# An attention and mixture-of-experts kernel on one core: expert weights halved in pieces of 512 columns, and the tables of the left rows begun after two batches

## The chip, the cores and the metric

One Trainium2 chip, one of its cores. The metric is the device time of one execution in microseconds. The kernel before was timed three times: 989.87, 989.98 and 990.37 us, median 989.98 us. A traced execution of it took 992.81 us, of which 991.0 us lie between its first and its last instruction (its span).

## What is computed

The reference has two stages. The first is attention through 49 agents, the second a mixture of eight experts of which each row uses one:

```python
a2k = sm(agents, k); agent_v = a2k @ v          # per batch: 49 x 128
x = sm(q, agents) @ agent_v                     # 4 batches x 11456 rows x 128
logits = x @ w_gate; e_idx = argmax(logits)     # 8 experts
gate_w = softmax(logits)[e_idx]
eom = sigmoid(x @ w_output_gate)[e_idx]
for e in range(8):                              # rows with e_idx == e
    out[rows] = gate_w * eom * (relu(x[rows] @ w1[e]) @ w2[e])
```

`w1` is 128 x 1024 and `w2` 1024 x 128 for each expert. Matmuls that must be exact beyond fp16 are made as a sum of fp16 products: a value is split in a high half (rounded to fp16) and a low half (the rest), and the product of the two low halves is dropped.

## The kernel before, in words

**Two ways to a result.** In each batch one expert is chosen by far the most often (`choose`, L886). All rows of the batch go through that expert in the main stream: 92 tiles of up to 512 rows (23 a batch), each with 16 `h` products of 512 columns (`mm1`, L1283), eight relu steps that split `h` in halves `hh` (ScalarE) and `hl` (VectorE) (`relu`, L1307), and `y` products (`mm2`, L1317), which ScalarE and VectorE add up, GpSimd scales by a factor for each row and SyncE stores (`finish`, `store`). The rows that chose another expert, the left rows, are gathered afterwards, computed in tiles of 128 with their own expert's weights, and scattered over the output. They come in two phases (`PHASES`, L30): phase 0 is batches 0 and 1, with 12 tiles, phase 1 is batches 2 and 3, with one.

**The left rows, step by step.** `q_rest` and `q_tail` (L1110, L1217) leave for each batch the running counts of rows for each expert (`cumd`, `tot`) and set `counted` to the number of batches done. `left_prepare(ph)` (L1731) then makes, in this order, the table of the phase (`left_table`, L1436: which tile has which expert, some 23 short VectorE instructions, three small matmuls, three stores), loads the averages of the agents (`left_averages`, L1653) and runs the index work for groups of four tiles (`left_index`, L1505: which rows, by two rounds of indirect DMAs on GpSimd's queue, first of `cumd` and then of the saved exponentials `efd`). Phase 0 begins when three batches are counted, phase 1 when all four are and phase 0's index work is over (`prepared`). `left_static` (L1763) is two streams ("ways"), each of which takes every second tile; in a way a tile's front (`left_load`, L1636, and `left_front`, L1665: double the exponentials on VectorE, transpose `let` and product `lx` on TensorE, halves `lxs`) begins once the tile before it in this way is finished, and its back (`left_back`, L1687: 24 `lh` matmuls, relu, 16 `ly` matmuls, two scalings) follows. The back of phase 1's tile also waits for the end of the main stream (`ended`, L1788). `left_scatter` (L1797) writes a tile's rows out by an indirect DMA.

**Halves.** The left rows need all eight experts' weights in halves. `halves` (L966) makes them, one expert after another, beside the main stream: load `w1` and `w2` of the expert (`hw`), squares with an accumulated sum on ScalarE (`hd`, `hsq`), a sum over partitions by a matmul with ones (`hr`), a power of two as scale (`hb`, `hs`), then for each of the two weights: multiply by the scale in place (ScalarE, fp32, 1024 columns), copy to fp16 (ScalarE, 1024), subtract (GpSimd, 1024, fp32 minus fp16 to fp16), store. Experts 0 to 2 may begin once the first batch's weights are ready, 3 to 5 with the second's, 6 and 7 with the third's; `choose` waits while an expert is in the making, and left rows begin only when all eight are made.

**What sets the order.** No engine's order is found by hand. The program is written as generators ("streams", `spawn`) that ask for one instruction at a time; a planner with a model of costs (`Clock`, L56) walks through time and grants a request when its operands are ready by the model. Streams with a smaller priority number are asked first: -1 for what opens the next batch, 0 for relu and finish, 1 for the phase 0 preparation, 2 by default, 3 for the halves and the scatters, 4 for fronts and scores, 5 for the ways. The order on each engine is fixed when the program is built; on the chip each engine goes through its own list and waits on semaphores.

Of the kernel before, what the change touches and what calls it, by code (L numbers as in the profile page):

```python
# [7 lines left out]
F32 = mybir.dt.float32  # L8
F16 = mybir.dt.float16
# [8 lines left out]
P = 128  # L18
# [250 lines left out]
def agent_attention_top1_moe(ctx, tc, qT, kT, v, aT, wg, wo, w1, w2, cst, sides, out):  # L269
# [696 lines left out]
    def halves():  # L966

        for e in range(E):
            while not (clk.started and len(state) > e // 3 and "i12" in state[len(state) - 1]
                       and (len(state) < B and K.get(len(state), {"v": 0})["v"] < 8) and not urgent[0]):  # L970
                yield None
            halving[0] = True
            src, dst = [], []
            for x in (w1, w2):
                s = wk.tile([P, F], F32, name=f"hw{len(src)}_{e}", tag="w1t", bufs=2)
                yield from SY.q.dma_start(s, x[e])
                src.append(s)
            sq = wk.tile([P, 2], F32, name=f"hsq{e}", tag="hsq")
            for k in range(2):
                d = wk.tile([P, 2 * F], F16, name=f"hd{k}_{e}", tag="w2t", bufs=2)  # L980
                yield from ACT.q.activation(d[:, 0:F], src[k], AF.Square, accum_out=sq[:, k:k + 1])
                dst.append(d)
            yield from wait_free()
            r = bank(f"hr{e}")
            mark = hold()
            yield from PE.q.matmul(r[:, 0:2], ones, sq, start=True, stop=True)
            sb, s, si = (wk.tile([P, 2], I32, name=f"h{n}{e}", tag=f"h{n}") for n in ("b", "s", "si"))
            for k, x in enumerate((9, 15)):
                yield from DVE.q.tensor_scalar(sb[:, k:k + 1], r[:, k:k + 1].bitcast(I32), -0.5,
                                               float((190 + x << 23) - (1 << 23)), op0=ALU.mult, op1=ALU.add)  # L990
            release(mark)
            yield from DVE.q.tensor_scalar(s, sb, 0x7F000000 + 0x800000, None, op0=ALU.bitwise_and)
            yield from POOL.q.tensor_scalar(si, s, -1.0, float(254 << 23), op0=ALU.mult, op1=ALU.add)
            s, si = s.bitcast(F32), si.bitcast(F32)
            yield from POOL.q.tensor_tensor(wsi[:, e:e + 1], si[:, 0:1], si[:, 1:2], op=ALU.mult)
            for k, x in enumerate((w1p, w2p)):
                if k == 0:
                    hi, lo, full = dst[k][:, 0:F], dst[k][:, F:2 * F], src[k]
                else:
                    v4 = dst[k].rearrange("p (f h c) -> p f h c", h=2, c=C)  # L1000
                    hi, lo, full = v4[:, :, 0, :], v4[:, :, 1, :], src[k].rearrange("p (f c) -> p f c", c=C)
                yield from ACT.q.activation(full, full, AF.Copy, scale=s[:, k:k + 1])
                yield from ACT.q.copy(hi, full)
                yield from POOL.q.tensor_tensor(lo, full, hi, op=ALU.subtract)
                yield from SY.q.dma_start(x[e], dst[k])
            halved[0] = e + 1
            halving[0] = False
# [654 lines left out]
        while clk.now() < t:  # L1662
            yield None

    def left_front(nm, ef, xt, two, ie, av):  # L1665
        yield from DVE.q.tensor_tensor(xt, ef[:, 0:A].unsqueeze(1).broadcast_to([P, 2, A]),
                                       two.unsqueeze(2).broadcast_to([P, 2, A]), op=ALU.mult)
        yield from wait_free()
        t = bank(f"let{nm}")
        mark = hold()  # L1670
        yield from PE.q.transpose(t[0:2 * A, 0:P], xt.rearrange("p b k -> p (b k)"), idf)
        et = wk.tile([P, P], F32, name=f"let_sb{nm}", tag="l_et")
        yield from ACT.q.copy(et[0:2 * A], t[0:2 * A, 0:P])
        release(mark)
        yield from wait_free()
        x = bank(f"lx{nm}")
        mark = hold()
        yield from PE.q.matmul(x[:, 0:P], av[0:2 * A], et[0:2 * A], start=True, stop=True)
        xs = wk.tile([P, 2, P], F16, name=f"lxs{nm}", tag="l_xs")
        yield from ACT.q.copy(xs[:, 0, :], x[:, 0:P])  # L1680
        yield from DVE.q.scalar_tensor_tensor(xs[:, 1, :], x[:, 0:P], 1.0, xs[:, 0, :], op0=ALU.mult, op1=ALU.subtract)
        release(mark)
        g = wk.tile([P, 1], F32, name=f"lg_{nm}", tag="l_g", bufs=3)
        yield from DVE.q.tensor_tensor(g, ef[:, A:A + 1], ie, op=ALU.mult)
        return xs, g
# [45 lines left out]
    def left_prepare(ph):  # L1731

        b0, nb, nst, _ = PHASES[ph]
        while counted[0] < (3 if ph == 0 else B) or ph and not prepared[0]:
            yield None
        if ph == 0:
            yield from SY.q.dma_start(ls, sides)
        yield from left_table(ph)
        averaged[ph] = yield from left_averages(ph, f"{ph}")
        i = 0  # L1740
        for j, n in enumerate((4, 4, 4) if nst > 2 else (nst,)):
            big = None
            if nst > 2:
                while B - 1 not in K or K[B - 1]["s"] < min(3 * j + 3, NU):
                    yield None
                big = wk.tile([P, min(24, NCOL - 24 * j), A2], F32, name=f"big{ph}_{i}", tag=f"S{j}", bufs=1)
                big = big.rearrange("p t a -> p (t a)")

            def got(k, t, ti, tu, ef, oa, xt, two, ie, i=i):
                ready[ph, i + k] = t, ti, k, tu[:, k:k + 1], ef[:, k, :], oa[:, k, :], xt[:, k], two[:, k, :], ie[:, k:k + 1]  # L1750
            yield from left_index(ph, i, n, f"s{ph}_{i}", got, big)
            i += n
        prepared[0] = True
# [9 lines left out]
    def left_static(way):  # L1763


        while way and (B - 1 not in K or K[B - 1]["v"] < NU):
            yield None
        todo = [(ph, k) for ph, x in enumerate(PHASES) for k in range(x[2])][way::WAYS]
        ops = {}
        finished = [0]  # L1770

        def fronts():
            for i, (ph, k) in enumerate(todo):
                while (ph, k) not in ready or i > finished[0] or halved[0] < E:
                    yield None
                t, ti, kk, _, ef, _, xt, two, ie = ready[ph, k]
                yield from pause(t - clk.now())
                w1t, w2t = yield from left_load(ph, ti, kk, f"{ph}_{k}", left_place)
                yield from pause(max(clk.ready[x.name] for x in (w1t, w2t)) - clk.now())
                xs = yield from left_front(f"{ph}_{k}", ef, xt, two, ie, averaged[ph])  # L1780
                ops[ph, k] = xs, w1t, w2t

        spawn(fronts(), LEFT - 1)
        for ph, k in todo:
            while (ph, k) not in ops:
                yield None
            xs = ops.pop((ph, k))
            while ph == len(PHASES) - 1 and not ended[0]:  # L1788
                yield None
            tu, _, oa = ready[ph, k][3:6]  # L1790
            yield from left_back(f"{ph}_{k}", *xs, oa, ("lh", "ev")[way])
            for x in (f"lw1{ph}_{k}", f"lw2{ph}_{k}"):
                scored((x, 0, 0))
            left.append((ph, oa, tu))
            finished[0] += 1
# [21 lines left out]
                return stop.value  # L1817

    AHEAD = 5
    LASTQ = 0  # L1820
    WARM = 6000
    WARM0 = 36
# [6 lines left out]
    spawn(clear(), 5)  # L1829
    spawn(small_products(), 4)  # L1830
    for ph in range(len(PHASES)):
        spawn(left_prepare(ph), 1 - ph)
    for way in range(WAYS):
        spawn(left_static(way), LEFT)
    spawn(left_scatter(), 3)
    spawn(halves(), 3)
    main_stream()

    DVE.tensor_tensor(more, over[:, 0:1], over[:, 1:2], op=ALU.max)
# [1 line left out]
    with tc.For_i(0, some, 1):  # L1841
        for ph, (b0, nb, nst, rows) in enumerate(PHASES):
            nr = nc.values_load(nti[ph][0:1, 0:1], min_val=0, max_val=rows,
                                skip_runtime_bounds_check_because="at most one tile per 128 tokens and one per group")
            with tc.For_i(nst, nr, 1) as i:
                ti, tu, ef, oa, xt, two, ie = drain(left_index(ph, i, 1, f"d{ph}"))
                w1t, w2t = drain(left_load(ph, ti, 0, f"d{ph}"))
                av = drain(left_averages(ph, f"d{ph}"))
                xs = drain(left_front(f"d{ph}", ef[:, 0, :], xt[:, 0], two[:, 0, :], ie, av))
                drain(left_back(f"d{ph}", xs, w1t, w2t, oa[:, 0, :]))  # L1850
                drain(left_store(ph, oa[:, 0, :], tu[:, 0:1]))

# [62 lines left out]
```

## Time and profile before

| what | value |
|---|---|
| median of three runs | 989.98 us |
| the profiled execution, and its span | 992.81 us, 991.0 us |
| TensorE (PE) busy | 949.1 us, 96% of the span |
| VectorE (DVE) busy | 828.3 us, 84% |
| ScalarE (ACT) busy | 632.2 us, 64% |
| GpSimd (POOL) busy | 394.9 us, 40% |
| mean granted TensorE clock | 0.991 |
| the 16 DMA queues, mean rate | 166 GB/s |

A row of a group gives line, engine, operation, output and inputs, shape and count, then the time in which any instruction of the group ran, the mean of one in ns, and the idle time in front of it with what ended it. Nearly every row says L219, since one helper issues all queued instructions; the names of the tiles tell them apart. TensorE's matmuls are pipelined, so rows of single matmuls are longer than the distance from one to the next.

### The profile page before, as it was taken

To read this page: it belongs to the slowest core of one execution; us is meant where nothing else is said; L and a number is where in the kernel's file an instruction comes from. 1 tells how busy PE (TensorE), PEld (TensorE's weight loads), DVE (VectorE), ACT (ScalarE), POOL (GpSimd) and SP (SyncE) were. 2 spreads that over 40 slices of the span, in tenths; PEclk is the share of its full clock that TensorE was granted. 3 is DMA by queue.
4 is the path that set the end of the run, shared out by engine and by line. 5 is a ranking of instruction groups with operands and counts; after the bars stand their busy time and mean duration, and the time that the engine had idled before them with its cause. 6 is when DMAs were issued, how large, how long until landed. Compare 5 with 4: busy or idle time off the path is not lost.

```text
span 991.0 us, 37853 instructions
## 1 busy us (share of the span) xinstructions
PE 949.1 (96%) x15819; PEld 716.8 (72%) x15819; DVE 828.3 (84%) x2245; ACT 632.2 (64%) x1459; POOL 394.9 (40%) x661
## 2 busy tenths in 40 slices
PE   9999999999999999999989999999999999999994
PEld 7867777777777777777767777777777666767783
DVE  2878888989878988989878889889889898898872
ACT  2378677766767886657767666666556565655542
POOL 1124366652243666432335454432226334533321
PEclk9999999999999999999999999999999999999997
DMA  9996958647469865444676554444332525524341
GB/s 324 302 322 181 249 157 219 183 136 167 152 183 267 245 180 166 129 146 142 179 245 208 161 153 144 145 125 148 84 101 77 134 73 151 133 86 133 94 138 62
DMA packets 112609, 164.10 MB, mean 166 GB/s; under 512 B 62961, under 2 KB 71110, under 8 KB 112432
## 3 DMA queue, kind: packets, MB, share of 16 engines
q1 hardware_dynamic: 111184, 160.18, 54.6%
q8 instruction: 125, 2.05, 0.9%
q0 software_dynamic: 1248, 1.44, 0.8%
q14 instruction: 52, 0.43, 0.2%
HBM read 97.91 MB, written 43.49 MB: 143 GB/s over the span
## 4 chain that ended last, share of the span: by engine, by line
PE 70%; DVE 18%; ACT 7%; DMA 2%; issue 2%; POOL 0%; POOLq 0%; SPq 0%; ACTq 0%; DVEq 0%
PE y L219 36%; PE h L219 17%; DVE hl L219 10%; ACT hh L219 4%; PE ks L219 3%; PE qs L219 3%; PE av L219 2%; PE warm L219 2%; PE ly L219 1%; DVE os L219 1%; ACT hd L219 1%; PE avT L219 1%; PE lh L219 1%; DVE a L219 1%; PE lg L219 1%
## 5 line engine op out<-in xcount | busy, mean ns | idle before, releaser
L219 PE MATMUL y<-vv,hh 128*128 128x256 f16 (+1 forms) x2880 | 526.1, 274 | 12.0 <-DVE lL L219 3.9
L219 DVE SCALAR_TENSOR_TENSOR hl<-h,hh 128x512 f16<-128x512 f32 (+1 forms) x736 | 450.5, 667 | 75.6 <-ACT hh L219 74.0
L219 PE MATMUL y<-vv,hl 128*128 128x128 f16 (+1 forms) x2880 | 500.9, 220 | 3.0 <-DVE hl L219 2.0
L219 ACT ACTIVATE hh<-h 128x512 f16<-128x512 f32 (+1 forms) x736 | 372.6, 593 | 177.9 <-PE h L219 177.9
L219 PEld LDWEIGHTS <-hh 128*128 128x128 f16 (+1 forms) x2880 | 283.6, 98 | 54.8 <-issue 13.7
L219 PEld LDWEIGHTS <-hl 128*128 128x128 f16 (+1 forms) x2880 | 284.8, 99 | 16.7 <-issue 8.2
L219 PE MATMUL h<-x_ld,w 128*128 128x512 f16 (+1 forms) x1472 | 254.5, 376 | 3.2 <-DVE hl L219 2.7
L219 PEld LDWEIGHTS <-w 128*128 128x128 f16 x1472 | 83.5, 95 | 116.6 <-issue 79.3
L219 POOL TENSOR_TENSOR os<-os,smt 128x512 f32<-128x512 f32 (+1 forms) x91 | 94.4, 1038 | 95.4 <-DVE os L219 65.4
L219 ACT COPY ys<-y 128x256 f32<-128x256 f32 x179 | 68.2, 381 | 73.8 <-PE y L219 72.4
L219 DVE TENSOR_TENSOR os<-y,ys 128x256 f32<-128x256 f32 x179 | 74.1, 414 | 17.9 <-ACT ys L219 17.3
L219 POOL TENSOR_TENSOR e<-ef,e 128x392 f16<-128x392 f32 (+1 forms) x48 | 44.3, 923 | 64.1 <-ACT e L219 63.8
L219 POOL TENSOR_TENSOR ev<-S,km_o 128x400 f32<-128x400 f32 (+1 forms) x36 | 32.9, 914 | 54.5 <-PE av L219 52.3
L219 PE MATMUL ks<-at,k_ld 128*32 128x50 f32 (+1 forms) x2252 | 47.2, 213 | 0.9 <-DMA k_ld<-kT 0.7
L219 PEld LDWEIGHTS ks<-at,k_ld 128*32 128x32 f32 (+1 forms) x2252 | 40.6, 117 | 10.3 <-issue 7.0
L219 PE MATMUL qs<-at,q_ld 128*32 128x50 f32 (+1 forms) x2736 | 43.5, 210 | 2.0 <-issue 2.0
L219 PEld LDWEIGHTS qs<-at,q_ld 128*32 128x32 f32 (+1 forms) x2736 | 36.5, 111 | 12.0 <-issue 10.8
L219 POOL TENSOR_SCALAR smt<-lT,i 128x8 f32<-128x8 f32 (+1 forms) x48 | 15.6, 326 | 64.7 <-DVE lT L219 27.5
L219 POOL TENSOR_TENSOR hd<-hw,hd 128x1024 f16<-128x1024 f32 x16 | 34.2, 2137 | 14.0 <-ACT hd L219 14.0
L219 ACT COPY S<-ks 128x400 f32<-128x400 f32 (+1 forms) x48 | 23.7, 498 | 22.5 <-PE ks L219 22.5
L219 POOL TENSOR_TENSOR sm<-sm,ev 128x400 f32<-128x400 f32 (+1 forms) x33 | 32.2, 977 | 11.2 <-ACT ev L219 11.2
L219 PE MATMUL lh<-lxs,lw_ld 128*128 128x128 f16 x312 | 33.7, 225 | 1.8 <-ACT lxs L219 0.7
(294 smaller groups left out, 1127.3 us busy)
## 6 DMA issues: line engine op xcount, KB each, us to landing
v_ld<-v SPq DMA_DIRECT2D x44, 512.0 KB, 4.9
q_ld<-qT SPq DMA_DIRECT2D x44, 512.0 KB, 4.1
out<-os SPq DMA_DIRECT2D x88, 256.0 KB, 3.1
k_ld<-kT SPq DMA_DIRECT2D x43, 512.0 KB, 5.3
efd<-ef SPq DMA_DIRECT2D x44, 200.0 KB, 3.6
x_ld<-x_ld SPq DMA_DIRECT2D x132, 64.0 KB, 3.9
hw<-w SPq DMA_DIRECT2D x16, 512.0 KB, 7.1
lw_ld<-w1p SPq DMA_DIRECT2D x13, 512.0 KB, 4.5
```

The costliest lines, as they stand in the source:

```text
L219: return getattr(self.eng, op)(*a, **k)
```

## The change

Four edits.

1. `halves` works on pieces of 512 columns. A piece gets its own square (ScalarE) and its own column of a sum tile with four columns, which two matmuls add up in place of one. The scaling in place on ScalarE and the copy to fp16 become one ScalarE instruction, which reads the fp32 weights, multiplies by the scale and writes the high half; the fp32 product for the subtraction is made by GpSimd (`tensor_scalar`, in place) ahead of its subtraction. The stream's priority goes from 3 to 6.
2. `left_prepare` of phase 0 begins when two batches are counted, with priority 3 in place of 1. After the table it waits until the weights of the last batch are made (`i12` of batch 3), then loads the averages, and spawns the index work as a stream of its own with priority 1. Phase 1's order stays as it was.
3. The doubling of the exponentials leaves `left_front` for a step of its own, `left_double`, ahead of the load of the tile's weights; a pause of 1 us by the model's clock stands after it.
4. The tiles `let_sb` and `lxs` take buffers of the rings `w1t` and `w2t` in place of rings of their own.

```diff
-            sq = wk.tile([P, 2], F32, name=f"hsq{e}", tag="hsq")
+            sq = wk.tile([P, 4], F32, name=f"hsq{e}", tag="hsq")
             for k in range(2):
-                yield from ACT.q.activation(d[:, 0:F], src[k], AF.Square, accum_out=sq[:, k:k + 1])
+                for hf in range(2):
+                    cs = slice(hf * 512, (hf + 1) * 512)
+                    yield from ACT.q.activation(d[:, cs], src[k][:, cs], AF.Square, accum_out=sq[:, 2 * hf + k:2 * hf + k + 1])
...
-            yield from PE.q.matmul(r[:, 0:2], ones, sq, start=True, stop=True)
+            yield from PE.q.matmul(r[:, 0:2], ones, sq[:, 0:2], start=True, stop=False)
+            yield from PE.q.matmul(r[:, 0:2], ones, sq[:, 2:4], start=False, stop=True)
...
-                yield from ACT.q.activation(full, full, AF.Copy, scale=s[:, k:k + 1])
-                yield from ACT.q.copy(hi, full)
-                yield from POOL.q.tensor_tensor(lo, full, hi, op=ALU.subtract)
+                for hf in range(2):
...
+                    yield from ACT.q.activation(hi, full, AF.Copy, scale=s[:, k:k + 1])
+                    yield from POOL.q.tensor_scalar(full, full, s[:, k:k + 1], None, op0=ALU.mult)
+                    yield from POOL.q.tensor_tensor(lo, full, hi, op=ALU.subtract)
...
-    def left_front(nm, ef, xt, two, ie, av):
+    def left_double(ef, xt, two):
         yield from DVE.q.tensor_tensor(xt, ef[:, 0:A].unsqueeze(1).broadcast_to([P, 2, A]),
                                        two.unsqueeze(2).broadcast_to([P, 2, A]), op=ALU.mult)
+
+    def left_front(nm, ef, xt, ie, av):
...
-        et = wk.tile([P, P], F32, name=f"let_sb{nm}", tag="l_et")
+        et = wk.tile([P, F], F32, name=f"let_sb{nm}", tag="w1t", bufs=2)[:, 0:P]
...
-        xs = wk.tile([P, 2, P], F16, name=f"lxs{nm}", tag="l_xs")
+        xs = wk.tile([P, 2 * F], F16, name=f"lxs{nm}", tag="w2t", bufs=2)[:, 0:2 * P].rearrange("p (k c) -> p k c", k=2)
...
-        while counted[0] < (3 if ph == 0 else B) or ph and not prepared[0]:
+        while counted[0] < (2 if ph == 0 else B) or ph and not prepared[0]:
             yield None
         if ph == 0:
             yield from SY.q.dma_start(ls, sides)
         yield from left_table(ph)
+        while ph == 0 and "i12" not in state.get(B - 1, {}):
+            yield None
         averaged[ph] = yield from left_averages(ph, f"{ph}")
+        spawn(left_indices(ph), 1 - ph)
+
+    def left_indices(ph):
+
+        nst = PHASES[ph][2]
...
                 yield from pause(t - clk.now())
+                yield from left_double(ef, xt, two)
+                t = clk.vt["DVE"] + 1000.0
                 w1t, w2t = yield from left_load(ph, ti, kk, f"{ph}_{k}", left_place)
+                yield from pause(t - clk.now())
...
+    EARLYP = 3
...
-        spawn(left_prepare(ph), 1 - ph)
+        spawn(left_prepare(ph), EARLYP if ph == 0 else 0)
...
-    spawn(halves(), 3)
+    spawn(halves(), 6)
```

The loop over more tiles than planned at the program's end (L1841 on) is changed in the same way; it runs no turn with these inputs.

More of the change, by code (lines that the diff above doesn't have):

```diff
@@ L996, in halves @@
             for k, x in enumerate((w1p, w2p)):
[L997 to L1001, printed above, removed]
-                yield from ACT.q.activation(full, full, AF.Copy, scale=s[:, k:k + 1])
-                yield from ACT.q.copy(hi, full)
-                yield from POOL.q.tensor_tensor(lo, full, hi, op=ALU.subtract)
+                for hf in range(2):
+                    cs = slice(hf * 512, (hf + 1) * 512)
+                    full = src[k][:, cs]
+                    if k == 0:
+                        hi, lo = dst[k][:, cs], dst[k][:, F + hf * 512:F + hf * 512 + 512]
+                    else:
+                        v4 = dst[k].rearrange("p (f h c) -> p f h c", h=2, c=C)[:, 4 * hf:4 * hf + 4]
+                        hi, lo, full = v4[:, :, 0, :], v4[:, :, 1, :], full.rearrange("p (f c) -> p f c", c=C)
+                    yield from ACT.q.activation(hi, full, AF.Copy, scale=s[:, k:k + 1])
+                    yield from POOL.q.tensor_scalar(full, full, s[:, k:k + 1], None, op0=ALU.mult)
+                    yield from POOL.q.tensor_tensor(lo, full, hi, op=ALU.subtract)
                 yield from SY.q.dma_start(x[e], dst[k])
@@ L1777, in fronts @@
                 yield from pause(t - clk.now())
+                yield from left_double(ef, xt, two)
+                t = clk.vt["DVE"] + 1000.0
                 w1t, w2t = yield from left_load(ph, ti, kk, f"{ph}_{k}", left_place)
+                yield from pause(t - clk.now())
                 yield from pause(max(clk.ready[x.name] for x in (w1t, w2t)) - clk.now())
-                xs = yield from left_front(f"{ph}_{k}", ef, xt, two, ie, averaged[ph])
+                xs = yield from left_front(f"{ph}_{k}", ef, xt, ie, averaged[ph])
                 ops[ph, k] = xs, w1t, w2t
@@ L1848, in agent_attention_top1_moe @@
                 av = drain(left_averages(ph, f"d{ph}"))
-                xs = drain(left_front(f"d{ph}", ef[:, 0, :], xt[:, 0], two[:, 0, :], ie, av))
+                drain(left_double(ef[:, 0, :], xt[:, 0], two[:, 0, :]))
+                xs = drain(left_front(f"d{ph}", ef[:, 0, :], xt[:, 0], ie, av))
                 drain(left_back(f"d{ph}", xs, w1t, w2t, oa[:, 0, :]))
```

## The prediction

> **What bounds it now.** I read the page first: the engines' busy shares and the chain that ended last.
>
> ```profile
> span 991.0 us, 37853 instructions
> PE 949.1 (96%) x15819; PEld 716.8 (72%) x15819; DVE 828.3 (84%) x2245; ACT 632.2 (64%) x1459; POOL 394.9 (40%) x661
> PE 70%; DVE 18%; ACT 7%; DMA 2%; issue 2%; POOL 0%; POOLq 0%; SPq 0%; ACTq 0%; DVEq 0%
> ```
>
> TensorE is busy 96% of the span and makes 70% of the chain. While the main stream runs, a microsecond is won only by taking work or a wait from TensorE. So I next asked where TensorE is not full: busy time by windows, and around the end the timeline and the chain.
>
> ```profile
> 944.00:964.00 20.00, 19.66 (x241) 17.12 (x238) 15.09 (x57) 8.92 (x25) 6.23 (x7) 1.00 0.41 135
> 964.16:974.25 10.09, 7.04 (x85) 5.63 (x84) 5.03 (x14) 4.54 (x11) 1.01 (x2) 1.00 0.41 143
> 974.25:983.00 8.75, 5.56 (x43) 4.12 (x43) 2.16 (x6) 2.09 (x5) 1.97 (x2) 0.80 0.01 2
> 963.94 0.22 PE L219 MATMUL y<-vv,hl 128*96 128x128 f16 x1
> 974.29 0.30 PE let L219
> 976.15 2.37 PE lh L219 x23
> 978.52 2.21 PE ly L219 x16
> 982.11 0.66 POOL out L219
> ```
>
> A windows row gives the stretch, its length, then PE, PEld, DVE, ACT and POOL busy. The main stream's last matmul ends at 963.94 + 0.22 = 964.16. Up to there TensorE is full (19.66 of 20). Then come 991.0 - 964.16 = 26.8 us of tail. Its first 10.1 us finish left tiles 10 and 11 of phase 0, with TensorE busy 7.04; after 974.25 phase 1's single tile goes alone through front, `lh`, `ly` and the scatter. From its first `lh` with both halves (976.15) to the end of the span it takes 14.85 us. That part must follow the main stream in any case, because its back waits for `ended`; what stands in front of it need not.
>
> **Why the left rows are late.**
>
> ```profile
> L219 DVE COPY tot<-cum x1: 786/786/786, 467.0 to 467.0; 128x8 f32<-128x8 f32 x1
> L219 PE MATMUL pexc<-tot,kc x4: 182/262/283, 689.7 to 926.1; 128*128 128x16 f32 x4
> L219 DVE TENSOR_TENSOR i<-s_si x1: 151/151/151, 693.6 to 693.6; 128x1 f32<-128x1 f32 x1
> L219 DVE TENSOR_SCALAR over<-t x2: 143/144/144, 719.2 to 936.7; 128x1 f32<-128x1 f32 x2
> L219 POOL DMA_INDIRECT big<-efd,ltu_8s x4: 997/1023/1072, 919.5 to 924.5; - x4
> 937.44 0.29 PE L219 MATMUL let<-kc,big 128*98 128x128 f32 x1
> 953.80 0.37 ACT L219 ACTIVATE big<-ly,lg 128x128 f32<-128x128 f32 x1 [1.37 <-PE ly L219]
> 962.67 0.27 PE L219 MATMUL let<-kc,big 128*98 128x128 f32 x1
> ```
>
> A tile row has the count, min/median/max in ns, and the first and last start. Phase 0's table starts at 689.7, once three batches are counted, and ends at 719.2 (`over`); only then the index work of the groups runs, one after another, and the last gather of the third group starts at 924.5. A tile in its way takes from 937.44 (front of tile 8) to 962.67 (front of tile 10), 25.2 us, of which the back ends at 953.80. So what is late at the end was late at 719.2.
>
> **Edit 2, the early table.** Two batches are counted at 467.0, so the table (29.5 us, 689.7 to 719.2) can be made some 220 us earlier. But the index work then waits for `i12` of batch 3, which stands at 693.6. So 719.2 - 693.8 = 25.4 us is what reaches the groups, not 220. I shift all that follows by this: tile 10's front from 962.67 to 937.3, with the same 25.2 us phase 1's tile's front to 962.5, its first full `lh` 1.86 later (974.29 to 976.15 now), 964.4. Tile 11, one way beside it, comes in as much earlier. Phase 1's table also moves: it started at 926.1 because of `prepared` and can start with the fourth batch's count and the shifted gather (924.5 - 25.4 = 899.1), so its index work isn't late either. The table's small instructions move into 467 to 500, into VectorE and TensorE lists that are full there too, and leave a place as full; its load and three stores move ahead on SyncE's queue with it. I count that as nothing, bounds 1.5 us either way (23 VectorE instructions of 0.144, the `over` row, are 3.3 us; half of it reaching TensorE).
>
> The work that leaves the tail is not gone. TensorE's 7.04 us, and what precedes phase 1's main part (5.56 - 2.37 - 2.21 = 1.0, from the third windows row and the chain), go into the main stream, which has no holes by the first windows row: +8.0 us at its end. Bounds: 0, if holes take it all, and 8.0.
>
> **Edit 3, doubling ahead.** In the main stream TensorE waits at `let` for the doubling.
>
> ```profile
> PE let L219 <- issue: 1.8, 4, 1.1
> PE let L219 <- DVE big L219: 1.4, 2, 0.9
> 974.29 0.29 PE L219 MATMUL let<-kc,bigs 128*98 128x128 f32 x1 [1.06 <-issue]
> 967.66 0.31 PE L219 MATMUL let<-kc,big 128*98 128x128 f32 x1 [0.91 <-DVE big L219]
> ```
>
> Totals of us, times, longest. Two of the six lie in the tail (1.06 and 0.91); 3.2 - 1.97 = 1.2 us lie in the main stream. With the doubling done before the weights are asked for, they go: -1.2 us. What is next late there is the weights' landing, which the front waits for by plan already.
>
> **Edit 1, the halves.** Rows for each engine, one kind of instruction each (the last three of ScalarE's are of other tiles, in the forms that the change uses).
>
> ```profile
> L219 ACT ACTIVATE hw<-hw,hs 128x1024 f32<-128x1024 f32 x16 | 18.8, 1176 | 0.0
> L219 ACT ACTIVATE hd<-hw 128x1024 f16<-128x1024 f32 x16 | 17.2, 1088 | 0.0
> L219 ACT CAST hd<-hw 128x1024 f16<-128x1024 f32 x16 | 17.1, 1070 | 0.1
> L219 ACT ACTIVATION_READ_ACCUMULATOR hd<-hw 128x1 f32 x16 | 3.6, 227 | 0.0
> L219 ACT ACTIVATE vv<-w2t,s_s 128x512 f16<-128x512 f32 x8 | 5.9, 732 | 0.6 <-DVE sx_s L219 0.6
> L219 ACT ACTIVATE vv<-w2t 128x512 f16<-128x512 f32 x8 | 5.0, 637 | 0.1
> L219 ACT ACTIVATION_READ_ACCUMULATOR vv<-w2t 128x1 f32 x8 | 1.6, 206 | 0.0
> L219 POOL TENSOR_TENSOR hd<-hw,hd 128x1024 f16<-128x1024 f32 x16 | 34.2, 2137 | 14.0 <-ACT hd L219 14.0
> L219 POOL TENSOR_TENSOR os<-os,smt 128x512 f32<-128x512 f32 x88 | 92.2, 1048 | 87.9 <-DVE os L219 57.9 <-DVE a L219 21.9 <-DVE ei L219 4.1
> L219 POOL COPY sm<-ev 128x400 f32<-128x400 f32 x3 | 1.6, 517 | 0.3 <-ACT ev L219 0.3
> PE y L219 <- ACT S L219: 3.6, 3, 1.3
> 479.72 1.08 ACT L219 ACTIVATE hd<-hw 128x1024 f16<-128x1024 f32 x1
> 481.60 0.27 PE L219 MATMUL y<-vv,hh 128*128 128x256 f16 x1 [1.15 <-ACT S L219]
> 481.87 0.28 PE L219 MATMUL hr<-hsq,ones 128*128 128x2 f32 x2
> 482.01 0.20 PE L219 MATMUL lg<-gs,x_ld 128*128 128x36 f16 x2
> ```
>
> ScalarE, for one weight: 1088 + 227 + 1176 + 1070 = 3561 ns now; two pieces of 637 + 206 + 732 = 3150 then. Over 16 weights 6.6 us less, on an engine that is 64% busy: nothing by itself. What counts is the blocking. At 479.72 a square held ScalarE for 1.08 us and its accumulator for 0.22; the score copy `S` behind it came late, and TensorE stood 1.15 us before the next `y`, which waited for it. There are three such waits, 3.6 us. A piece blocks 637 + 206 = 0.84 us instead of 1.31, so each shrinks by 0.47: -1.4 us, bounds 0 (two pieces in a row) and -3.6.
>
> TensorE gets eight more `hr` products; one takes 482.01 - 481.87 = 0.14 us of its list: +1.1 us, bounds 1.1 and 2.2 (0.28 each).
>
> GpSimd gets 32 multiplications of 512 columns. None is in the trace. Bounds are the copy of 400 columns, 0.52, and the two-input product of 512, 1.05; I take 0.6, close to the copy, which like it reads one tensor. That is 19 us more (17 to 34), plus subtractions in halves (32 x 1.05 = 34, as now), on an engine 40% busy. The new step lengthens one expert's making by some 2 us, and the lower priority by more; behind it wait only the fronts, which begin after all eight experts are made. I take 0. The Trainium skill ("GPSIMD Engine Reference", Elementwise, side-by-side cycle accounting) gives 769 ns as measured for a tight one-input loop over 512 elements; by it the 32 would be 24.6 us, and the sum would not change.
>
> What GpSimd does can hold VectorE, though:
>
> ```profile
> 492.62 2.01 DVE L219 SCALAR_TENSOR_TENSOR a<-eo,a 128x8 f32<-128x8 f32 x1
> 492.49 2.13 POOL L219 TENSOR_TENSOR hd<-hw,hd 128x1024 f16<-128x1024 f32 x1
> ```
>
> An instruction over 8 columns took 2.01 us and ended as the subtraction did. Split in two, one such hold is at most 1.05 us; the multiplications add new ones. I set these against each other at 0, bounds -2 and +10 (the slower rival, below). The Trainium skill ("GPSIMD Engine Reference", Specifications) says that GpSimd's SBUF interface is shared with VectorE and contends with instructions in a two-port mode or with two SBUF inputs. That fits this pair and speaks against adding GpSimd work.
>
> Edit 4 takes buffers from rings that nothing else uses once all experts are made and batch 3 has its weights: 0.
>
> **The sum.** End of the main stream: 964.16 + 8.0 - 1.2 - 1.4 + 1.1 = 970.7. Phase 1's tile is ready at 964.4 by the shift, so its back follows at once: 970.7 + 14.85 = 985.5 us of span, 5.5 less than 991.0. The profiled execution took 992.81 us (1.8 around the span), so 987.3 for one like it; against the median of 989.98, 2.8 below the profiled one, I forecast 984.5 us.
>
> **Rivals.**
>
> *The shift melts (0.18).* It must hold through three groups. The front of phase 1's tile has 970.7 - 964.4 = 6.3 us to spare; once less than 19.1 of the 25.4 us arrives, each lost microsecond is one of tail, and at 13.6 the gain is gone. For it: the index work now falls into 694 to 719, where the last batch's weights are made, and where VectorE, 84% busy over the span, has much to do besides. Against: the same stretch held the table before. Then the end is 988 to 991, say 989.
>
> *GpSimd holds VectorE (slower, 0.13).* In the three stretches of halving each of 32 multiplications catches a VectorE instruction and holds it for half its own length, 0.3 us, and all of that reaches TensorE through late `hl`: 32 x 0.3 = 9.6 us, so 984.5 + 9.6 = 994.1. It decides from 5.5 us on, that is once over 0.17 us for each multiplication arrives at TensorE. For it: the pair above. Against: `hl`, most of VectorE's work, reads the fp32 side from PSUM, and the pieces of the subtraction hold half as long.
>
> *TensorE has room (0.07).* Holes between matmuls, which busy time does not show, take the 8.0 us: 984.5 - 8.0 = 976.5.
>
> That the change doesn't do what it says, the early table bringing nothing since the index work waits for something else at 694, is the first of these with no shift at all.
>
> **The numbers.** The forecast, 984.5, has 0.62: with bounds of its own from 980 to 988. The range is to hold it, the melted shift and a part of either end: 980 to 991 leaves out the slower case and most of the roomy one. A measurement here tells 0.2%, 2 us, from no change: faster is under 988.0, 0.69 from the forecast and the roomy case; the same, 988 to 992, has the melted shift's 0.18; slower 0.13.
>
> **What would show it.** Right: `tbs` of the first group near 695, third group's gathers near 899, tile 11's scaling before the last `y`, the main stream's end near 970, and no second `let` of phase 0 after it. `ACT S` waits under 3 us, GpSimd up by 17 to 34 us. Wrong: a `let` of phase 1 after the end of the main stream; many 8-column VectorE instructions of 0.5 us and more beside GpSimd's multiplications; a main stream that ends later than 972.

## The result and the profile after

The changed kernel takes 980.35 us (median of four runs, 978.36 to 981.23); the kernel before, on the same chip, 989.92 us (989.62 to 990.37). The ratio is 0.9900, interval 0.9883 to 0.9917: 9.6 us less, where 5.5 were forecast. The profiled execution took 980.56 us, 0.2 above its median, while the profiled one of before lay 2.8 above the median of its first three runs. So the two traces differ by more, 991.0 - 978.8 = 12.2 us of span, and part of that isn't the change: the mean granted clock is 0.991 in the one and 0.996 in the other.

The page of the changed kernel, its first lines and the chain:

```profile
span 978.8 us, 38020 instructions
PE 942.6 (96%) x15867; PEld 715.2 (73%) x15867; DVE 821.4 (84%) x2245; ACT 623.0 (64%) x1491; POOL 443.9 (45%) x709
PE 67%; DVE 12%; ACT 7%; POOL 6%; issue 5%; DMA 2%; SPq 0%; POOLq 0%; ACTq 0%; DVEq 0%
```

TensorE has 48 instructions more and yet 949.1 - 942.6 = 6.5 us less busy time. Its idle time fell from 991.0 - 949.1 = 41.9 to 36.2, 5.7 us less. These two are the whole 12.2. GpSimd has 49.0 us more than before.

The end of the kernel, by windows, first of the kernel before, with its tail in one row up to the last scatter:

```profile
944.00:964.16 20.16, 19.82 (x242) 17.28 (x239) 15.09 (x57) 8.92 (x25) 6.39 (x7) 1.00 0.41 134
964.16:982.20 18.04, 12.61 (x128) 9.75 (x127) 7.18 (x20) 6.63 (x16) 2.41 (x4) 0.91 0.23 81
982.20:991.00 8.80, 0.00 (x0) 0.00 (x0) 0.00 (x0) 0.00 (x0) 0.57 (x1) 0.56 0.03 9
```

The same three stretches of the changed kernel:

```profile
951.00:964.90 13.90, 13.88 (x177) 12.68 (x175) 7.81 (x22) 5.82 (x20) 4.03 (x4) 1.00 0.14 53
964.90:969.80 4.90, 2.90 (x39) 2.26 (x36) 2.40 (x6) 2.05 (x5) 0.16 (x2) 1.00 0.07 20
969.80:978.80 9.00, 0.00 (x0) 0.00 (x0) 0.00 (x0) 0.00 (x0) 0.92 (x1) 0.62 0.03 9
```

The tail shrinks from 26.8 to 13.9 us: the middle stretch from 18.04 to 4.90, and the scatter's 9 us stay. TensorE's idle time in the middle stretch falls from 18.04 - 12.61 = 5.43 to 2.00 us. PEclk there is 1.00 in place of 0.91. The main stream ends where it did, at 964.8 against 964.16, though it holds tiles 10 and 11 and phase 1's front now.

Rows of the tiles that the shift goes through, in the changed kernel (count, min/median/max, first and last start):

```profile
L219 DVE TENSOR_SCALAR over<-t x2: 139/139/139, 507.2 to 911.4; 128x1 f32<-128x1 f32 x2
L219 PE MATMUL tbs<-big,ones x6: 193/236/276, 695.5 to 830.0; 128*128 128x32 f32 x6
L219 POOL DMA_INDIRECT big<-efd,ltu_8s x4: 996/1055/1113, 890.2 to 896.0; - x4
L219 PE MATMUL let<-kc,bigs x1: 273/273/273, 960.1 to 960.1; 128*98 128x128 f32 x1
```

The table ends at 507.2 in place of 719.2; the index work starts at 695.5 (695 forecast); the third group's last gather starts at 896.0 in place of 924.5, so 28.5 us earlier where 25.4 were forecast; phase 1's front stands at 960.1 in place of 974.3, ahead of the end of the main stream.

The new GpSimd rows and the smaller subtraction, from the groups:

```profile
L219 POOL TENSOR_SCALAR hw<-hw,hs 128x512 f32<-128x512 f32 x32 | 51.1, 1598 | 33.6 <-ACT hd L219 33.6
L219 POOL TENSOR_TENSOR hd<-hw,hd 128x512 f16<-128x512 f32 x32 | 37.2, 1163 | 1.3
```

One multiplication takes 1.6 us, beyond the 0.52 to 1.05 that I gave as bounds.

TensorE's waits in the first halving stretch (60 to 190 us; total, times, longest), before:

```profile
PE y L219 <- ACT S L219: 1.3, 1, 1.3
PE y L219 <- DVE lL L219: 0.7, 1, 0.7
PE y L219 <- DVE os L219: 0.7, 1, 0.7
PE h L219 <- DVE hl L219: 0.7, 3, 0.2
PE y L219 <- DVE hl L219: 0.4, 1, 0.4
PE y L219 <- DVE hb L219: 0.3, 1, 0.3
PE lg L219 <- DVE os L219: 0.2, 1, 0.2
```

and after:

```profile
PE ks L219 <- DMA k_ld<-kT: 0.7, 1, 0.7
PE y L219 <- DVE hl L219: 0.4, 1, 0.4
PE lg L219 <- DVE os L219: 0.3, 1, 0.3
PE h L219 <- DVE hl L219: 0.2, 1, 0.2
PE y L219 <- DVE os L219: 0.2, 1, 0.2
```

Waits that VectorE ended were 3.0 us and are 1.1. That is a term that I hadn't counted at all. Counted in the same way over the three halving stretches (60 to 190, 265 to 390, 470 to 550), they fall from 5.4 to 1.3 us, those ended by `S` from 3.6 to 2.7. All waits of TensorE in these stretches, whatever ended them, fall from 11.0 to 6.9 us.

**Theory and rivals after the result.** Theory: edits 2 to 4 bring what the sum says, about 5.2 us, and edit 1 brings the missing 4, by way of VectorE-ended waits in the halving stretches. Rivals: the table brings more than the sum says and edit 1 nothing; or the new priority, by another order of the whole program, brings the rest. Within edit 1 the squares, the scaling, the piece length and the move of the product to GpSimd are four candidates.

### The profile page after: what moved, and what is told of

Read it like the earlier page. It is cut to its first block, busy times and chain, and to the rows that moved or that the text cites. A ratio compares the mean times of both kernels' runs of the same rounds, so it can differ in the third digit from the quotient of the medians.

```text
span 978.8 us, 38020 instructions
## 1 busy us (share of the span) xinstructions
PE 942.6 (96%) x15867; PEld 715.2 (73%) x15867; DVE 821.4 (84%) x2245; ACT 623.0 (64%) x1491; POOL 443.9 (45%) x709
## 4 chain that ended last, share of the span: by engine, by line
PE 67%; DVE 12%; ACT 7%; POOL 6%; issue 5%; DMA 2%; SPq 0%; POOLq 0%; ACTq 0%; DVEq 0%
PE y L219 34%; PE h L219 16%; DVE hl L219 7%; ACT hh L219 4%; PE ks L219 3%; PE qs L219 3%; PE av L219 2%; PE warm L219 2%; PE ly L219 1%; PE lh L219 1%; POOL os L219 1%; PE avT L219 1%; DVE os L219 1%; POOL hw L219 1%; DMA hw<-w 1%
## 5 line engine op out<-in xcount | busy, mean ns | idle before, releaser
L219 POOL TENSOR_SCALAR hw<-hw,hs 128x512 f32<-128x512 f32 x32 | 51.1, 1598 | 33.6 <-ACT hd L219 33.6
L219 POOL TENSOR_TENSOR e<-ef,e 128x392 f16<-128x392 f32 (+1 forms) x48 | 42.1, 878 | 43.4 <-ACT e L219 43.2
L219 POOL TENSOR_TENSOR ll<-lL,rr 128x128 f32<-128x128 f32 (+1 forms) x48 | 19.3, 401 | 44.1 <-DVE rr L219 35.5
L219 POOL TENSOR_TENSOR hd<-hw,hd 128x512 f16<-128x512 f32 x32 | 37.2, 1163 | 1.3
```

Of the source, the lines that this page charges most:

```text
L219: return getattr(self.eng, op)(*a, **k)
```

## The experiments

Each is compared with the kernel before, timed beside it on the same chip. There are three such groups, with the kernel before at 989.95, 990.73 and 995.86 us. The last chip is 0.6% slower, so across groups ratios are compared, not times. A difference in us is that of the medians; the ratio is taken over all executions and can lie a little beside it. Its interval is about 0.2%, 2 us, to either side. Traces are of single executions, and the planner makes a new order for each variant.

**Edit 1 alone.** The kernel before with the body of `halves` of the changed kernel, the first part of the diff above, and its priority.

```diff
-            sq = wk.tile([P, 2], F32, name=f"hsq{e}", tag="hsq")
+            sq = wk.tile([P, 4], F32, name=f"hsq{e}", tag="hsq")
...
-    spawn(halves(), 3)
+    spawn(halves(), 6)
```

> Edit 1 alone on the kernel before: weights halved in pieces of 512, GpSimd multiplication, stream priority 6. The sum on record (-1.4 for shorter ScalarE blocking, +1.1 for eight more hr products) gives about 989.6 us, no measurable change. A rival theory, read from the two traces (batch 0 of the main stream is 4.6 us shorter after the change): the halves are what was left out of the sum, and this kernel is near 985.5 us. The theory that GpSimd's longer work holds VectorE gives 994 us or more.

Measured: 985.41 us (982.6 to 986.32) against 989.95, ratio 0.9943 (0.9922 to 0.9965): -4.5 us. The sum's value for edit 1, -0.3, falls. The waits of this kernel in the three halving stretches: 1.1 us ended by VectorE (5.4 before) and 2.8 by `S` (3.6). Waits on a load and on `issue` grow by 0.7, so all of them together fall from 11.0 to 6.6 us, by 4.4. Eight more `hr` products of 0.14 take 1.1 back: 3.3 of the 4.5 measured. The trace of before also has TensorE's clock at half for 3.4 us at 280.1, within a halving stretch, and this one has not. So the waits bear out the order of size and no more.

**Edit 2 alone.** The early table in the kernel before, with `left_indices` and `EARLYP` as in the change.

```diff
-        while counted[0] < (3 if ph == 0 else B) or ph and not prepared[0]:
+        while counted[0] < (2 if ph == 0 else B) or ph and not prepared[0]:
...
+        while ph == 0 and "i12" not in state.get(B - 1, {}):
+            yield None
         averaged[ph] = yield from left_averages(ph, f"{ph}")
+        spawn(left_indices(ph), 1 - ph)
```

> Edit 2 alone on the kernel before: table at two batches, index work at the last batch's weights. The sum on record for this edit: tail 12 us shorter, main stream 8.0 us longer, so about 986.0 us. If TensorE takes the moved left work in holes between matmuls: 982 us or less. If the shift melts: 989 us. In the trace the main stream should end near 972, with phase 1's front before it.

Measured: 985.94 us (984.52 to 987.12) against 989.95, ratio 0.9948 (0.9929 to 0.9966): -4.0 us. Without edits 1 and 3 the sum is 964.16 + 8.0 + 14.85 = 987.0 of span, 4.0 less than 991.0. The amount is as forecast, within an interval of 3.4 to 7.0 us, but the way there isn't. The tail's windows of this kernel:

```profile
962.20:976.30 14.10, 8.87 (x87) 7.23 (x86) 6.18 (x15) 4.70 (x12) 3.04 (x3) 0.88 0.10 33
976.30:985.20 8.90, 0.00 (x0) 0.00 (x0) 0.12 (x2) 0.00 (x0) 0.98 (x1) 0.54 0.03 7
```

and its fronts:

```profile
L219 PE MATMUL let<-kc,big x12: 271/287/417, 786.3 to 968.4; 128*98 128x128 f32 x12
L219 PE MATMUL let<-kc,bigs x1: 287/287/287, 965.3 to 965.3; 128*98 128x128 f32 x1
```

The main stream ends at 962.2, not 972, and the tail keeps two fronts (965.3 and 968.4) and 23.0 us. Its two tiles overlap, though, and hold TensorE busy 8.87 of 14.1 us. So 12.61 - 8.87 = 3.7 us of TensorE's work left the tail, the tail is 26.8 - 23.0 = 3.8 us shorter, and the main stream ends 2.0 us earlier, not 8.0 later. At most 1.7 of these 2.0 are the clock, which is at half once for 3.4 us in this main stream and twice in that of before. That the main stream took the 3.7 us in without getting longer is a reading of two single traces; why it could is open.

**Edits 2 to 4, without the halves.** The changed kernel with the old body of `halves` and priority 3.

```diff
-            sq = wk.tile([P, 4], F32, name=f"hsq{e}", tag="hsq")
+            sq = wk.tile([P, 2], F32, name=f"hsq{e}", tag="hsq")
...
-    spawn(halves(), 6)
+    spawn(halves(), 3)
```

> The changed kernel with edit 1 taken back (edits 2, 3 and 4 stay). If edit 1 is worth what the sum says (0.3 us), this is within 1 us of the changed kernel, 980.7 us. If edit 1 is worth the 4 us by which the forecast missed, this is near 984.5 us.

Measured: 984.69 us (983.66 to 984.89) against 989.95, ratio 0.9939 (0.9921 to 0.9956): -5.3 us. The sum without edit 1's terms is 964.16 + 8.0 - 1.2 + 14.85 = 985.8 of span, 5.2 less than 991.0. Windows around its end:

```profile
955.00:968.40 13.40, 13.38 (x171) 12.22 (x169) 7.45 (x22) 5.44 (x19) 3.90 (x4) 1.00 0.14 51
968.40:973.40 5.00, 3.03 (x41) 2.38 (x38) 2.40 (x6) 2.06 (x5) 0.26 (x2) 1.00 0.07 20
973.40:981.90 8.50, 0.00 (x0) 0.00 (x0) 0.00 (x0) 0.00 (x0) 0.95 (x1) 0.61 0.03 9
```

Here the form of the forecast holds: a full main stream up to 968.4 (970.96 by the sum) and a short tail, 13.5 us. Against the early table alone, on the same chip, edits 3 and 4 bring 985.94 - 984.69 = 1.25 us; 1.2 were forecast. The executions of the two kernels overlap (984.52 to 987.12, and 983.66 to 984.89), so this fits the forecast and does not show it.

**Edit 3 alone.** The kernel before with `left_double` ahead of the weights and the pause.

```diff
+                yield from left_double(ef, xt, two)
+                t = clk.vt["DVE"] + 1000.0
                 w1t, w2t = yield from left_load(ph, ti, kk, f"{ph}_{k}", left_place)
+                yield from pause(t - clk.now())
```

> Edit 3 alone on the kernel before: doubling ahead of the load, rings as before. The sum gives -1.2 us in the main stream, so 988.7 us, and no wait of TensorE at let for the doubling. The rival: these waits were only idle time that something else would have ended, no change, 989.9 us.

Measured: 988.27 us against 989.95, ratio 0.9981 (0.9965 to 0.9996). But this kernel does not return the right output (it is off by 4.4%), and one of its eleven executions took 1169.52 us, the others 985.57 to 990.21. Why is not known, and its time is no measure of edit 3. What is left is the pair above.

**Edit 1 in parts.** Three kernels: the squares in pieces alone, the scaling in pieces (with the new GpSimd multiplication) alone, and the priority alone, each on the kernel before. The edits in this order:

```diff
+                for hf in range(2):
+                    cs = slice(hf * 512, (hf + 1) * 512)
+                    yield from ACT.q.activation(d[:, cs], src[k][:, cs], AF.Square, accum_out=sq[:, 2 * hf + k:2 * hf + k + 1])
```

```diff
+                for hf in range(2):
...
+                    yield from ACT.q.activation(hi, full, AF.Copy, scale=s[:, k:k + 1])
+                    yield from POOL.q.tensor_scalar(full, full, s[:, k:k + 1], None, op0=ALU.mult)
+                    yield from POOL.q.tensor_tensor(lo, full, hi, op=ALU.subtract)
```

```diff
-    spawn(halves(), 3)
+    spawn(halves(), 6)
```

> From edit 1 only the squares in pieces (and the second hr product), on the kernel before; scaling, copy and subtraction in 1024 columns and priority 3 as before. Edit 1 as a whole gave -4.5 us. If long squares on ScalarE, 1.31 us with the accumulator, are what makes TensorE wait: most of it here, about 987 us or less. If it is the scaling, copying and subtracting: no change, 990 us.

> From edit 1 only the second half, on the kernel before: one ScalarE operation and a GpSimd multiplication and subtraction for each piece of 512; squares in 1024 columns and priority 3 as before. If the 2.14 us subtraction, which holds VectorE, or the 1.18 + 1.07 us on ScalarE cost TensorE's waits: about 987 us or less. If the squares do: no change, 990 us; then the longer work on GpSimd costs nothing either. If that work holds VectorE: above 992 us.

> From edit 1 only the priority of the halves, 6 in place of 3, on the kernel before. The theory that piece length matters: no change, 990 us within 1. The rival that asking the halves last keeps them out of the way of scores and score copies: some of the 4.5 us, 987 us. It also tells what a mere change of the order, with no work changed, is worth.

Measured against 990.73 us: the squares 990.54, ratio 1.0000 (0.9983 to 1.0016); the scaling 986.76, ratio 0.9953 (0.9936 to 0.9970); the priority 990.63, ratio 0.9981 (0.9968 to 0.9995). The scaling carries edit 1. The priority is worth 0.1 us by the medians and 0.3% at most by its interval, about what can be told here. The pieces of the square, on which I had put the -1.4 us of shorter `S` waits, bring nothing by themselves.

The traces of the parts warn against going by one kind of wait. In the three halving stretches the squares alone do shorten the `S` waits, from 3.6 to 1.4 us, and VectorE's, from 5.4 to 2.0. But waits on `issue` grow from 2.0 to 4.1, 1.1 us on ScalarE's `eo` come in, and nothing is gained. With the scaling alone `S` keeps 3.3 of 3.6 us, VectorE's waits fall to 2.5, and 4.0 us are gained. All waits together are 11.0 us before, 8.8 with the squares, 8.1 with the scaling and 6.6 with edit 1.

**The squares, from the other side.** The changed kernel with whole squares and one `hr` product.

```diff
-                for hf in range(2):
-                    cs = slice(hf * 512, (hf + 1) * 512)
-                    yield from ACT.q.activation(d[:, cs], src[k][:, cs], AF.Square, accum_out=sq[:, 2 * hf + k:2 * hf + k + 1])
+                yield from ACT.q.activation(d[:, 0:F], src[k], AF.Square, accum_out=sq[:, k:k + 1])
```

> The changed kernel with the squares of the halves in 1024 columns again and one hr product in place of two (eight products of 0.14 us fewer). squares_only showed no gain from these pieces: within 1 us of the changed kernel's 980.4 us, or up to 1 us less. If the shorter ScalarE blocks matter once scaling is in pieces too: 982 us or more.

Measured: 987.13 us against 995.86, ratio 0.9906 (0.9892 to 0.9919), beside 0.9900 of the changed kernel. That looks as if the pieces were not missed, but the granted clock speaks against it: over its five executions it is 0.997 on average, over the ten of before beside it 0.992, and 0.5% of 987 us is up to 5 us. In its trace TensorE waits 10.5 us in the halving stretches, 6.9 in the changed kernel, and is idle 42.7 us of the span in place of 36.2. So what the square's pieces are worth next to the split scaling stays open.

**Does GpSimd's total time count?** The changed kernel with the same multiplication written with two tensor inputs, the scale broadcast over the columns.

```diff
-    yield from POOL.q.tensor_scalar(full, full, s[:, k:k + 1], None, op0=ALU.mult)
+    yield from POOL.q.tensor_tensor(src[k][:, cs], src[k][:, cs], s[:, k:k + 1].broadcast_to([P, 512]), op=ALU.mult)
```

> The changed kernel with GpSimd's multiplication written with two tensor inputs (the scale broadcast along the row) in place of a scalar pointer. In the trace of the change the multiplication took 1.58 us of 512 columns, where a two-input product of as many takes 1.05. So 32 x 0.53 = 17 us less on GpSimd. If GpSimd's time beside the main stream costs nothing: within 1 us of the changed kernel's 980.4 us. If it holds VectorE and TensorE: 977 us.

Measured: 982.19 us against 990.73, ratio 0.9904 (0.9888 to 0.9921). Its GpSimd row from the groups:

```profile
L219 POOL TENSOR_TENSOR hw<-hw,hs 128x512 f32<-128x512 f32 x32 | 33.5, 1046 | 40.9 <-ACT hd L219 40.9
```

17.6 us of GpSimd's time less, and the ratio is the same within 0.2%. GpSimd's total load isn't on the path.

**Pieces without the move, and the move without pieces.** Both on the kernel before. The first keeps both ScalarE operations and puts no product on GpSimd, but works in pieces of 512:

```diff
+                for hf in range(2):
...
+                    yield from ACT.q.activation(full, full, AF.Copy, scale=s[:, k:k + 1])
+                    yield from ACT.q.copy(hi, full)
+                    yield from POOL.q.tensor_tensor(lo, full, hi, op=ALU.subtract)
```

The second has the one ScalarE operation and GpSimd's product, over 1024 columns:

```diff
-                yield from ACT.q.activation(full, full, AF.Copy, scale=s[:, k:k + 1])
-                yield from ACT.q.copy(hi, full)
+                yield from ACT.q.activation(hi, full, AF.Copy, scale=s[:, k:k + 1])
+                yield from POOL.q.tensor_scalar(full, full, s[:, k:k + 1], None, op0=ALU.mult)
                 yield from POOL.q.tensor_tensor(lo, full, hi, op=ALU.subtract)
```

> On the kernel before: scaling in place, copy (both on ScalarE) and subtraction (GpSimd) in pieces of 512 columns, no GpSimd multiplication; squares and priority as before. ScalarE's and GpSimd's total work stays, each instruction is half as long. scaling_only gave -4.0 us. If piece length is what counts (ScalarE blocked 0.6 to 0.7 us at a time in place of 1.1 to 1.2, VectorE held at most 1.2 in place of 2.1): about 986.5 us. If the saved ScalarE operation counts: no change.

> On the kernel before: one ScalarE operation of 1024 columns (scale and copy in one) and GpSimd's multiplication and subtraction in 1024 columns (some 3.1 and 2.1 us); squares and priority as before. If the saved ScalarE operation counts: about 986.5 us. If piece length counts: no change, or slower, since GpSimd's instructions get longer; if GpSimd holds VectorE as long as they run, 992 us or more.

Measured against 995.86 us: in pieces 992.25, ratio 0.9960 (0.9942 to 0.9979); merged 1002.54, ratio 1.0059 (1.0041 to 1.0077). So the pieces bring about the gain of edit 1 by themselves (0.4%, 4.0 us), and fewer ScalarE operations with the move to GpSimd, unsplit, lose 0.6%. The waits of TensorE over the whole span of the merged kernel, its first three:

```profile
PE y L219 <- DVE os L219: 6.2, 5, 1.9
PE y L219 <- DVE lL L219: 5.5, 7, 1.8
PE y L219 <- ACT S L219: 2.4, 2, 1.3
```

and the same rows of the kernel before:

```profile
PE y L219 <- DVE lL L219: 3.9, 5, 1.0
PE y L219 <- ACT S L219: 3.6, 3, 1.3
PE y L219 <- DVE os L219: 2.4, 3, 1.1
```

The `S` waits are shorter, as the lighter ScalarE should make them, and the waits on VectorE's `os` and `lL` are 11.7 us in place of 6.3. One thing that makes VectorE late stands in the timeline of the merged kernel:

```profile
507.25 2.13 POOL L219 TENSOR_TENSOR hd<-hw,hd 128x1024 f16<-128x1024 f32 x1
507.80 2.01 DVE L219 TENSOR_TENSOR mx<-S,mx 128x400 f32<-128x400 f32 x1
```

and, with pieces, of the changed kernel:

```profile
543.95 1.16 POOL L219 TENSOR_TENSOR hd<-hw,hd 128x512 f16<-128x512 f32 x1
544.00 1.54 DVE L219 TENSOR_TENSOR mx<-S,mx 128x400 f32<-128x400 f32 x1
```

A running maximum that takes 0.55 us on average (the `mx` group of before) ends 0.43 us after the subtraction in both: 507.80 + 2.01 - 507.25 - 2.13, and 544.00 + 1.54 - 543.95 - 1.16. So it seems to stand still until the whole GpSimd instruction is over. The Trainium skill ("SBUF — State Buffer", Who interferes with whom) says that a VectorE instruction with two SBUF inputs contends with a GpSimd instruction that reads SBUF, and calls the contention an exclusive lock; these two pairs agree. So the length of a single GpSimd instruction is what VectorE can lose at a time.

That is not the whole of edit 1, though. The mean of this group, from the groups of before,

```profile
L219 DVE TENSOR_TENSOR mx<-S,mx 128x400 f32<-128x400 f32 (+1 forms) x40 | 21.9, 547 | 7.0 <-ACT S L219 6.9
```

of the merged kernel,

```profile
L219 DVE TENSOR_TENSOR mx<-S,mx 128x400 f32<-128x400 f32 (+1 forms) x40 | 29.2, 729 | 8.2 <-ACT S L219 8.1
```

and of the changed one,

```profile
L219 DVE TENSOR_TENSOR mx<-S,mx 128x400 f32<-128x400 f32 (+1 forms) x40 | 26.5, 661 | 8.0 <-ACT S L219 7.8
```

says that the changed kernel holds VectorE more than the kernel before, and still gains. The holds fit the loss of the merged form (part of which is the granted clock, on average 0.990 against 0.992 of before beside it); that they explain the gain of the pieces is not shown. `scaling_split` shortens ScalarE's instructions (1.18 and 1.07 us before) and GpSimd's at once; which of the two brings its 4.0 us wasn't separated and stays open.

**Is a later left row a later end?** The changed kernel with the index work of phase 0 held back by 12 us of the planner's clock.

```diff
+        if ph == 0:
+            yield from pause(12000.0)
         spawn(left_indices(ph), 1 - ph)
```

> The changed kernel with the index work of phase 0 held back by 12 us of the planner's clock. In the trace of the change phase 1's front was ready 2.6 us before the main stream's last matmul. If the theory of the tail is right (one microsecond of tail for each microsecond that this front comes late), some 9 us of the 12 go to the tail and some left work with them out of the main stream: 980.4 + 9 - 4 = 985 us. If the left rows have slack that the trace does not show: 981 us.

Measured: 984.28 us against 995.86, ratio 0.9875 (0.9860 to 0.9891). Not slower: its interval overlaps that of the changed kernel (0.9883 to 0.9917) and lies lower. The delay did arrive. The windows row of its tail up to the last scatter:

```profile
958.90:974.00 15.10, 11.46 (x105) 9.25 (x102) 5.70 (x16) 5.45 (x15) 4.05 (x4) 0.77 0.38 135
```

and phase 1's front, from the tile's rows:

```profile
L219 PE MATMUL let<-kc,bigs x1: 421/421/421, 966.2 to 966.2; 128*98 128x128 f32 x1
```

Phase 1's front starts at 966.2, 7.3 us after the main stream's end at 958.9, and the tail is 24.8 us. By the threshold in my first rival this costs some 7 us. It costs none: the main stream ends some 6 us earlier than the changed kernel's, since it holds less, and in the tail two tiles, one in each way, keep TensorE busy 11.46 of 15.1 us. That theory falls. It is the best ratio of the study; that it beats the changed kernel was not shown, since the two weren't timed on one chip.

## Why the prediction came out as it did

The direction was right, and the time lies inside the range, 0.35 us above its lower end. That it lies inside is luck: this end was set with a main stream that has room in mind, and not for a gain of 4 us in edit 1, for which the sum had 0.3. Step by step:

- **The early table and the doubling (edits 2, 3, 4): right in size together.** -5.3 us measured without the halves, -5.2 by the sum. Start of the index work, last gather and phase 1's front came close to the forecast. The `let` waits on VectorE's doubling are gone, though `y` now waits twice for `let_sb`, 1.2 us in all. The 8.0 us of work that enter the main stream fit the kernel without halves: its main stream ends 4.2 us later than before's, and with the 1.2 of edit 3 that makes 5.4. TensorE's clock was at half for 3.4 us twice in before's profiled main stream (280.1 and 730.7) and not in this one, which hides at most 2 x 1.7 us more: 5.4 to 8.8. For the table alone the right amount is luck: its tail got 3.8 us shorter and not 12, and its main stream didn't get 8.0 longer.
- **"I set these against each other at 0", for GpSimd and VectorE in edit 1: this is the step that was mis-sized.** The -0.3 for the whole edit became -4.5. I had looked for shorter waits under `ACT S` alone (-1.4 forecast, 3.6 to 2.7 measured). The square's pieces do shorten these when they stand alone, to 1.4, but other waits take their place and the time stays; the scaling in pieces is what gains. The waits in the same stretches that VectorE ended, 5.4 us, weren't in the sum. They fall to 1.3. Whether it is ScalarE's or GpSimd's shorter instructions that let VectorE be in time is open.
- **GpSimd's multiplication at 0.6 us, bounds 0.52 to 1.05: wrong,** 1.6. GpSimd got 49 us more, not 17 to 34. It cost nothing that can be told here, as the kernel with 17.6 us less shows, so the step "on an engine 40% busy" holds for GpSimd's total. It leaves out the length of one instruction, which the merged kernel shows to matter.
- **The slower rival, GpSimd holding VectorE:** not what happened, but holds there are: the running maximum's mean rises from 547 to 661 ns. With 1024 columns to an instruction it is 729 ns, and the kernel gets 0.6% slower than before.
- **"Each lost microsecond is one of tail" (first rival): refuted** by the delayed index work. Neither the tail's length nor TensorE's idle time in it measures the gain: the table alone gains its 4.0 us with a tail of 23.0 us, in whose middle stretch TensorE is idle for 14.10 - 8.87 = 5.23 us, against 5.43 before and 2.00 after.
- **The tail's 14.85 us** became 13.9: the half clock (0.51 from 976.5 to 979.9), under which its `lh` and `ly` rows had been read (2.37 and 2.21 us), isn't there any more; the 24 `lh` products take 1.50.

## What to carry to other kernels

When an edit shortens instructions of a side stream, add up all waits of the bound engine in the stretch where that stream runs, whichever engine ends them, and not only the wait that names the edited instruction: a wait that goes can come back under another name. Moving work to GpSimd was free of its total here, but split it: a VectorE instruction can stand until a single GpSimd instruction is over. Work taken from a tail has to go somewhere, and neither the tail's length nor the idle time in it tells what the move is worth; time the whole kernel. And before two ratios are called equal, compare the granted clocks behind them.

## What the runs showed of the hardware that was not expected

- GpSimd's product with a scale for each partition (one tensor input) takes 1598 ns over 512 columns, longer than the same product with two tensor inputs, 1046 ns, and than the subtraction, 1163.
- In the kernel before, TensorE's clock stood at half for 3.4 us after a gap of two microseconds. The gap and what follows, in windows:

```profile
277.20:279.30 2.10, 0.12 (x10) 0.00 (x2) 1.27 (x7) 0.67 (x4) 0.73 (x3) 1.00 0.43 164
280.10:283.50 3.40, 3.40 (x31) 2.79 (x28) 0.66 (x8) 0.27 (x1) 0.19 (x1) 0.50 0.82 201
```

The gap alone doesn't decide it. In the same execution the clock also fell at 730.7, with TensorE busy without a pause in the 3.4 us ahead:

```profile
727.30:730.70 3.40, 3.40 (x25) 2.10 (x25) 3.37 (x7) 2.59 (x6) 0.46 (x2) 1.00 0.42 80
730.70:734.10 3.40, 3.40 (x21) 2.35 (x19) 2.23 (x9) 1.27 (x3) 2.10 (x4) 0.50 0.34 87
```

And in the merged kernel a gap of nearly the same length is followed by the full clock:

```profile
521.70:523.70 2.00, 0.09 (x4) 0.01 (x1) 2.00 (x6) 1.07 (x5) 0.00 (x0) 1.00 0.75 256
523.70:527.10 3.40, 3.40 (x87) 2.36 (x87) 2.90 (x14) 1.69 (x4) 1.28 (x4) 1.00 0.22 60
```

The Trainium skill ("TensorE: Matmul & The Clock Gate", What's actually happening) puts the half clock after at least one idle window of about 3.4 us. Neither fall of the kernel before has an idle stretch of that length ahead of it; what brings them on is open.
